# Linear attention and a token MLP mixed by a gate: a new order of the first loads, and of VectorE's first statistics

## The chip, the cores and the metric

One core of one Trainium2 chip runs the kernel. The metric is the device time of one execution in microseconds. All times in the profile count from the start of the profiled span.

## The reference

x is [1, 2048, 512] in bfloat16. Two branches read it and a gate mixes them:

```python
g = sigmoid((x * gate_w).sum(-1))
# A: linear attention, 32 heads of 16, phi(t) = where(t > 0, t + 1, exp(t)) + 1e-6
q, k, v = split(x @ wqkv)
o = (phi(q) @ (phi(k)^T v)) / (phi(q) . sum(phi(k)) + 1e-6)
a = o @ wo
# B: MLP over the tokens, after a layernorm over the 512 features
h = (x - mean(x)) / sqrt(var(x) + 1e-5)
u = gelu(einsum("bsd,sf->bdf", h, w1) + b1)      # w1 [2048, 1792]
b = (einsum("bdf,fs->bds", u, w2) + b2)^T        # w2 [1792, 2048]
return g * a + (1 - g) * b
```

The first matmul of B sums over tokens: each tile of 128 tokens of the normalised x meets the 128 rows of w1 that belong to the same tokens.

## The kernel before

Tokens are cut into NT = 16 tiles of 128 (one token for each of 128 partitions). `xr[:, t, :]` holds tile t of x, `xh[:, t, :]` the normalised tile, `w1A[:, t, :]` the first 1024 columns of w1's tile t.

The kernel is written in the order in which each engine is to run (`pin` and `mm` keep program order on every engine, DMA queues included). It begins with stage one of B: for tiles 0 to 11 in turn, eight matmuls (one for each block of 128 columns of `w1A`, `mlp1` through `mm`, line 74) add to eight accumulators `accA`; the last four tiles are then done block by block, each followed by a gelu on ScalarE. After it come k, the sums for the attention, the other six blocks of stage one mixed with q, and last the second matmul of B and the output, tile by tile. TensorE runs 18 warm-up matmuls on a constant before any data is there.

What feeds the first stage:

- **Loads** (`load`, line 124). They go out on SP's queue unless another engine is named; three go out on ScalarE's own queue (ACT) at the start. On ACT: the rows of b1 into `b_rows`, then the first 128 columns of w1's tile 0, then those of tile 1, then a dummy Sqrt (line 137) that brings in the activation table. On SP: x tiles 0 and 1, the other 896 columns of w1's tile 0, then x tile 2, the other 896 columns of w1's tile 1, x tile 3, w1's tile 2, and so on in turns of x and w1. Behind w1's tile 4 come the rows of b2. VectorE clears `b_rows` (line 114) before either bias load.
- **Statistics on VectorE** (lines 194 to 235). For a tile: `ln_bn` (line 197, statistics of 512 columns at once, or of two halves of 256 for tiles 1 to 3), `ln_aggr` (line 200, aggregation; then a Sqrt on ScalarE, line 202, gives `sd`), `ln_apply` (line 208, reciprocal, and line 210, `xh`). The order is interleaved so that VectorE has work while ScalarE makes `sd`: for tiles 1 to 3 the first half's statistics of tile t, then `ln_apply(t - 1)`, the second half's statistics, `ln_aggr(t)`; from tile 4 on the full statistics of t, `ln_apply(t - 1)`, `ln_aggr(t)`. After tile 8 the bias rows are turned into columns on VectorE (line 232).

Of the kernel before, what the change touches and what calls it, by code (L numbers as in the profile page):

```python
# [15 lines left out]
def kernel(  # L16
# [13 lines left out]
    nc = tc.nc  # L30
    P = nc.NUM_PARTITIONS
# [7 lines left out]
    S, D = X.shape  # L39
    F = B_w1.shape[1]  # L40
    NT = S // P
    ND = D // P
    NF = F // P
# [4 lines left out]
    FA = NFA * P  # L48
    TAIL = 4

    x_view = X.rearrange("(t p) d -> p t d", p=P)
    o_view = O.rearrange("(t p) d -> p t d", p=P)
    wqkv_view = A_wqkv.rearrange("(k p) n -> p k n", p=P)
    w1_view = B_w1.rearrange("(t p) f -> p t f", p=P)
    w2_view = B_w2.rearrange("(f p) s -> p f s", p=P)
    b1_view = B_b1.rearrange("(f p) -> f p", p=P)
# [9 lines left out]
    def ptile(shape, dt, name):  # L66
        return persist.tile(shape, dt, name=name, tag=name)
# [9 lines left out]
    xr = ptile([P, NT, D], BF16, "xr")  # L77
# [17 lines left out]
    b_rows = ptile([32, P], BF16, "b_rows")  # L95
# [22 lines left out]
    w1A = wpool.tile([P, NT, FA], BF16, name="w1A", tag="w1st")  # L118
# [4 lines left out]
    def load(o, i, eng=None, **kw):  # L123
        pin((eng or nc.sync).dma_start(out=o, in_=i, **kw))  # L124

    def load_x(t0, t1):
        load(xr[:, t0:t1, :], x_view[:, t0:t1, :])

    def load_w1a(t):
        load(w1A[:, t, :], w1_view[:, t, 0:FA])  # L130


    tbl = work.tile([P, 1], FP32, name="tbl", tag="tbl", bufs=2)
    load(b_rows[0:NF, :], b1_view, nc.scalar)
    load(w1A[:, 0, 0:P], w1_view[:, 0, 0:P], nc.scalar)
    load(w1A[:, 1, 0:P], w1_view[:, 1, 0:P], nc.scalar)
    pin(nc.scalar.activation(out=tbl[:], in_=eps_t[:], func=ACT.Sqrt))

    load_x(0, 1)
    load_x(1, 2)  # L140
    load(w1A[:, 0, P:FA], w1_view[:, 0, P:FA])
    for t in range(1, NT):
        if t + 1 < NT:
            load_x(t + 1, t + 2)
        if t == 1:
            load(w1A[:, 1, P:FA], w1_view[:, 1, P:FA])
        else:
            load_w1a(t)
        if t == 4:
            load(b_rows[NF : NF + NT, :], b2_view)  # L150
    load(gw_b[:], gw_row_view.to_broadcast([P, D]))
    load(wk_sb[:], wqkv_view[:, :, D : 2 * D])
# [41 lines left out]
    def ln_bn(t, d0, d1, h, parts):  # L194
        if h == 0:
            stats[t] = work.tile([P, parts, BS], FP32, name="stats", tag=f"stats{parts}", bufs=4)
        pin(nc.vector.bn_stats(out=stats[t][:, h, :], in_=xr[:, t, d0:d1]))  # L197

    def ln_aggr(t):
        pin(nc.vector.bn_aggr(out=mv[:, t, :], in_=stats[t][:]))  # L200
        pin(
            nc.scalar.activation(
                out=sd[:, t : t + 1], in_=mv[:, t, 1:2], func=ACT.Sqrt, bias=eps_t[:], scale=1.0
            )
        )

    def ln_apply(t):
        pin(nc.vector.reciprocal(out=rstd[:, t : t + 1], in_=sd[:, t : t + 1]))
        pin(
            nc.vector.tensor_scalar(  # L210
                out=xh[:, t, :], in0=xr[:, t, :],
                scalar1=mv[:, t, 0:1], scalar2=rstd[:, t : t + 1],
                op0=ALU.subtract, op1=ALU.mult,
            )
        )

    HALVES = 4
    ln_bn(0, 0, D, 0, 1)
    ln_aggr(0)
    for t in range(1, NT):  # L220
        if t < HALVES:
            ln_bn(t, 0, D // 2, 0, 2)
            ln_apply(t - 1)
            ln_bn(t, D // 2, D, 1, 2)
        else:
            ln_bn(t, 0, D, 0, 1)
            ln_apply(t - 1)
        ln_aggr(t)
        if t == NT // 2:

            for p in range(0, P, 32):
                pin(nc.vector.transpose(out=b_cols[p : p + 32, :], in_=b_rows[:, p : p + 32]))
            pin(nc.vector.tensor_copy(out=b1_sb[:], in_=b_cols[:, 0:NF]))
            pin(nc.vector.tensor_copy(out=b2_sb[:], in_=b_cols[:, NF : NF + NT]))
# [322 lines left out]
    t = NT - 1  # L557
# [35 lines left out]
```

## Time and profile before

| | |
|---|---|
| time, median of 3 runs | 162.82 us (162.81 to 162.83) |
| the profiled execution: span from its first to its last instruction | 161.6 us |
| TensorE matmul busy | 157.1 us, 97% of the span |
| VectorE busy | 118.7 us, 73% |
| ScalarE busy | 53.0 us, 33% |
| mean TensorE clock granted | 0.998 |

The profile gives the span as the profiled execution's own time; the median of the runs is 1.2 us above it. Engines in the profile: PE is TensorE's matmuls, PEld its weight loads, DVE VectorE, ACT ScalarE, SPq and ACTq the queues on which SP and ScalarE issue DMAs. A duration of an issue (0.43 us for most) is that of the instruction that issues; the data lands later, and the page gives the time from the start of the issue to the landing. The chain of waits is followed back from the last instruction, at each step to what released it.

### The profile page before, as it was taken

The page shows a single profiled execution, that of the slowest core. Times are in us where ns is not written, and L with a number is a line of the kernel's source. Part 1 is how long each engine was busy: PE and PEld are TensorE (multiplying, and loading weights), DVE is VectorE, ACT ScalarE, POOL GpSimd, SP SyncE. Part 2 cuts the span into 40 slices and gives each one's busy share as a digit, 9 for nine tenths or more (in the row PEclk, how much of TensorE's full clock was granted, in tenths as well). Part 3 has the DMA queues.
Part 4 walks back from the last instruction along what each step waited for, and adds up shares of the span by engine and source line. Part 5 has one row for each costly group of instructions (what it writes and reads, how often), then busy time and mean ns, then how long its engine had stood idle before and what let it go on. Part 6 is the DMA issues. An engine that isn't in the chain of part 4 may idle for free.

```text
span 161.6 us, 2275 instructions
## 1 busy us (share of the span) xinstructions
PE 157.1 (97%) x820; PEld 72.9 (45%) x820; DVE 118.7 (73%) x279; ACT 53.0 (33%) x89; POOL 1.2 (1%) x8
## 2 busy tenths in 40 slices
PE   7899999999999999999999999999999999999993
PEld 5344444444444444444444444444444444444452
DVE  2799998959998998799895999999999980000002
ACT  3122226895243221435225970000008300550050
POOL 2000000000000000000000000000000000000000
PEclk9999999999999999999999999999999999999999
DMA  4999998444699540229953007826535925824421
GB/s 140 271 320 353 364 300 144 101 103 106 159 394 390 149 129 0 87 50 310 402 200 67 0 32 230 322 65 143 186 89 136 353 70 143 265 63 105 143 97 32
DMA packets 36966, 28.33 MB, mean 175 GB/s; under 512 B 20572, under 2 KB 31452, under 8 KB 36956
## 3 DMA queue, kind: packets, MB, share of 16 engines
q1 hardware_dynamic: 36368, 27.87, 57.0%
q10 hardware_dynamic: 588, 0.33, 0.7%
q8 instruction: 6, 0.10, 0.3%
q14 instruction: 4, 0.03, 0.1%
HBM read 19.28 MB, written 4.46 MB: 147 GB/s over the span
## 4 chain that ended last, share of the span: by engine, by line
PE 94%; DMA 3%; SPq 1%; DVE 0%; issue 0%; DVEq 0%
PE yps L74 39%; PE accA L74 16%; PE accB L74 13%; PE qacc L74 9%; PE Gps L74 9%; PE kacc L74 9%; DMA w1A<-in_B_w_dram 3%; SPq L124 1%; PE kvps L74 0%; DVE ot L537 0%; PE w2ps L74 0%; DVEq L537 0%
## 5 line engine op out<-in xcount | busy, mean ns | idle before, releaser
L74 PE MATMUL yps<-uT,w2h 128*128 128x512 bf16 (+2 forms) x238 | 49.2, 366 | 0.0
L74 PEld LDWEIGHTS <-w2h 128*128 128x128 bf16 x238 | 22.8, 98 | 25.9
L74 PE MATMUL accA<-xh,w1A 128*128 128x512 bf16 x128 | 28.0, 379 | 0.8 <-DVE xh L210 0.5
L530 ACT ACTIVATE ot<-yps,c,c 128x512 bf16<-128x512 f32 x15 | 11.6, 777 | 46.9 <-PE yps L74 35.5
L74 PE MATMUL accB<-xh,w1B 128*128 128x512 bf16 x96 | 21.5, 379 | 0.0
L537 DVE TENSOR_SCALAR ot<-yps,c,c 128x384 bf16<-128x384 f32 (+1 forms) x2 | 1.1, 545 | 25.5 <-PE yps L74 25.5
L74 PEld LDWEIGHTS <-w1A 128*128 128x128 bf16 x128 | 12.5, 98 | 16.1 <-DMA w1A<-in_B_w_dram 1.4
L74 PEld LDWEIGHTS <-xT 128*128 128x128 bf16 x128 | 12.4, 98 | 14.9 <-issue 0.2
L74 PE MATMUL kacc<-wk_sb,xT 128*128 128x512 bf16 x64 | 15.8, 379 | 0.0
L74 PE MATMUL Gps<-pk,xr 128*128 128x512 bf16 x64 | 15.8, 379 | 0.0
L74 PE MATMUL yps<-W2sb,pqT 128*128 128x512 bf16 (+2 forms) x68 | 14.6, 366 | 0.0
L74 PEld LDWEIGHTS <-w1B 128*128 128x128 bf16 x96 | 9.4, 98 | 11.3
L74 PE MATMUL qacc<-wq_sb,xT 128*128 128x512 bf16 x64 | 14.5, 379 | 0.0
L286 ACT ACTIVATE e<-qacc 128x512 bf16<-128x512 f32 x16 | 9.6, 597 | 12.2 <-DVE kvbdT L434 4.6
L286 ACT ACTIVATE e<-kacc 128x512 bf16<-128x512 f32 x16 | 9.2, 598 | 12.7 <-DVE pk L293 6.8
L197 DVE BATCH_NORM_STATS2 stats<-xr 128x6 f32<-128x512 bf16 (+1 forms) x19 | 11.1, 586 | 2.7 <-DMA xr<-in_A_x_dram 2.7
L288 DVE TENSOR_SCALAR e<-e 128x512 bf16<-128x512 bf16 x32 | 9.2, 288 | 4.6 <-ACT e L286 4.3
L406 DVE SCALAR_TENSOR_TENSOR pq<-pq,odds,rd 128x512 bf16<-128x512 bf16 x16 | 12.0, 752 | 0.6
L402 DVE TENSOR_REDUCE den<-prod 128x32 f32<-128x544 f32 x16 | 11.5, 720 | 0.6
L293 DVE SCALAR_TENSOR_TENSOR pk<-kacc,e 128x512 bf16<-128x512 f32 x16 | 11.1, 692 | 1.0
L293 DVE SCALAR_TENSOR_TENSOR pq<-qacc,e 128x512 bf16<-128x512 f32 x16 | 11.1, 692 | 0.6
L245 DVE CUSTOM_DVE_ANT_0 junk<-xr,gw_b 128x512 bf16<-128x512 bf16 x16 | 11.0, 689 | 0.4
(52 smaller groups left out, 95.0 us busy)
## 6 DMA issues: line engine op xcount, KB each, us to landing
w2h<-in_B_w_dram SPq DMA_DIRECT2D x3, 1792.0 KB, 7.5
w1A<-in_B_w_dram SPq DMA_DIRECT2D x14, 256.0 KB, 4.7
w1B<-in_B_w_dram SPq DMA_DIRECT2D x4, 768.0 KB, 6.2
xr<-in_A_x_dram SPq DMA_DIRECT2D x16, 128.0 KB, 4.1
q_dram<-pq SPq DMA_DIRECT2D x16, 128.0 KB, 3.7
out_dram<-ot SPq DMA_DIRECT2D x15, 128.0 KB, 1.8
w2h<-in_B_w_dram SPq DMA_DIRECT2D x1, 1280.0 KB, 6.5
wk_sb<-in_A_wqkv_dram SPq DMA_DIRECT2D x1, 512.0 KB, 6.5
```

The lines of the kernel that those rows point to most:

```text
L74: nc.tensor.matmul(o, lhsT=lhsT, rhs=rhs, start=start, stop=stop, **kw)
L124: pin((eng or nc.sync).dma_start(out=o, in_=i, **kw))
L197: pin(nc.vector.bn_stats(out=stats[t][:, h, :], in_=xr[:, t, d0:d1]))
L245: nc.vector.tensor_tensor_reduce(out=junk[:], in0=xr[:, t, :], in1=gw_b[:], scale=1.0, scalar=0.0, op0=ALU.mult, op1=ALU.add, accum_out=gp ...
L286: pin(nc.scalar.activation(out=e[:], in_=acc[:], func=ACT.Exp))
L288: nc.vector.tensor_scalar(out=e[:], in0=e[:], scalar1=1.0, scalar2=PHI_EPS, op0=ALU.min, op1=ALU.add)
L293: nc.vector.scalar_tensor_tensor(out=o, in0=acc[:], scalar=0.0, in1=e[:], op0=ALU.max, op1=ALU.add)
L402: pin(nc.vector.tensor_reduce(out=den[:], in_=prod[:], op=ALU.add, axis=AX.X))
L406: nc.vector.scalar_tensor_tensor(out=heads, in0=heads, scalar=odds[:, t : t + 1], in1=rd[:].unsqueeze(2).to_broadcast([P, NH, HEAD]), op0= ...
L530: nc.scalar.activation(out=ot[:, d0:d1], in_=yps[:, d0:d1], func=ACT.Identity, scale=c1[:, t : t + 1], bias=c2[:, t : t + 1],)
L537: nc.vector.tensor_scalar(out=ot[:, d0:d1], in0=yps[:, d0:d1], scalar1=c1[:, t : t + 1], scalar2=c2[:, t : t + 1], op0=ALU.mult, op1=ALU.add,)
```

## The change

Four edits, all in the first loads and in the order of the first statistics:

- x tile 0 comes as two halves: tokens 64 to 127 on ACT's queue, first there, in the place of the b1 rows; tokens 0 to 63 first on SP's queue.
- On SP the 896 columns of w1's tile 1 are issued ahead of x tile 2; the order behind is as it was (x tile 3, w1 tile 2, x tile 4, ...).
- The b1 rows are issued on SP, behind w1's tile 4 and ahead of the b2 rows.
- On VectorE, tile 1 is finished (`ln_apply(1)`) ahead of tile 2's statistics, and these are taken over all 512 columns at once. The first half of tile 3's statistics is still ahead of `ln_apply(2)`.

The instructions of TensorE, ScalarE (but for the first DMA) and GpSimd are as before and in the same order; VectorE has one instruction less.

```diff
-    load(b_rows[0:NF, :], b1_view, nc.scalar)
+    HP = P // 2
+    load(xr[HP:P, 0, :], x_view[HP:P, 0, :], nc.scalar)
     load(w1A[:, 0, 0:P], w1_view[:, 0, 0:P], nc.scalar)
     load(w1A[:, 1, 0:P], w1_view[:, 1, 0:P], nc.scalar)
     pin(nc.scalar.activation(out=tbl[:], in_=eps_t[:], func=ACT.Sqrt))
 
-    load_x(0, 1)
+    load(xr[0:HP, 0, :], x_view[0:HP, 0, :])
     load_x(1, 2)
     load(w1A[:, 0, P:FA], w1_view[:, 0, P:FA])
-    for t in range(1, NT):
+    load(w1A[:, 1, P:FA], w1_view[:, 1, P:FA])
+    load_x(2, 3)
+    for t in range(2, NT):
         if t + 1 < NT:
             load_x(t + 1, t + 2)
-        if t == 1:
-            load(w1A[:, 1, P:FA], w1_view[:, 1, P:FA])
-        else:
-            load_w1a(t)
+        load_w1a(t)
         if t == 4:
+            load(b_rows[0:NF, :], b1_view)
             load(b_rows[NF : NF + NT, :], b2_view)
@@
     ln_bn(0, 0, D, 0, 1)
     ln_aggr(0)
     for t in range(1, NT):
-        if t < HALVES:
+        if t == 2:
+            ln_apply(t - 1)
+            ln_bn(t, 0, D, 0, 1)
+        elif t < HALVES:
             ln_bn(t, 0, D // 2, 0, 2)
             ln_apply(t - 1)
             ln_bn(t, D // 2, D, 1, 2)
```

## The prediction

> **What bounds the kernel now.** I read the chain of waits first, then the list of waits of the first 20 us, then the timeline and the DMA issues of that stretch. Columns of the chain: start, duration, what.
>
> ```profile
> 2.67 4.65 DMA w1A<-in_B_w_dram
> 7.32 0.04 issue
> 7.37 25.86 PE accA L74 x119
> 33.23 4.32 PE kacc L74 x20
> ```
>
> From 7.37 us the chain holds nothing but TensorE until the last tile is finished. So the end is 7.37 plus work that the change leaves alone, and a shift of the first stage shifts the end one for one. Ahead of 7.37 stands one transfer: the last 896 columns of w1's tile 1 (call it w1/1), issued at 2.67, landed at 7.32. What TensorE can win is seen in its waits (total, times, longest):
>
> ```profile
> DVE stats L197 <- DMA xr<-in_A_x_dram: 2.7, 2, 1.9
> ...
> PEld L74 <- DMA w1A<-in_B_w_dram: 1.4, 2, 0.8
> ...
> PE accA L74 <- DVE xh L210: 0.5, 1, 0.5
> ...
> PE accA L74 <- DMA w1A<-in_B_w_dram: 0.3, 1, 0.3
> ```
>
> Two holes: 0.50 before the first matmul (normalised tile 0) and 0.31 at tile 1 (w1/1), 0.81 together; no version of this stage can win more. The timeline shows how close the next tiles are:
>
> ```profile
> 4.95 2.10 PE L74 MATMUL accA<-xh,w1A 128*128 128x512 bf16 x9 [0.50 <-DVE xh L210]
> ...
> 5.27 0.21 DVE L200 BATCH_NORM_AGGREGATE mv<-stats 128x2 f32<-128x12 f32 x1
> 5.44 0.43 DVE L197 BATCH_NORM_STATS2 stats<-xr 128x6 f32<-128x256 bf16 x1
> 5.51 0.30 ACT L202 ACTIVATE sd<-mv,eps_t 128x1 f32<-128x1 f32 x1 [1.26 <-DVE mv L200]
> 5.84 0.16 DVE L208 RECIPROCAL rstd<-sd 128x1 f32<-128x1 f32 x1
> 6.04 0.41 DVE L210 TENSOR_SCALAR xh<-xr,mv,rstd 128x512 bf16<-128x512 bf16 x1
> ...
> 7.75 0.43 DVE L197 BATCH_NORM_STATS2 stats<-xr 128x6 f32<-128x256 bf16 x1 [0.72 <-DMA xr<-in_A_x_dram]
> 8.10 0.15 DVE L208 RECIPROCAL rstd<-sd 128x1 f32<-128x1 f32 x1
> 8.28 0.41 DVE L210 TENSOR_SCALAR xh<-xr,mv,rstd 128x512 bf16<-128x512 bf16 x1
> ```
>
> A matmul takes 25.86/119 = 0.217, eight of them one tile. Tile 2 begins seven matmuls after 7.37, at 8.89, and its xh is ready at 8.28 + 0.41 = 8.69: 0.20 of room. The row at 7.75 says why so late: VectorE stood 0.72 for x tile 3, with tile 2's normalisation behind it in order. The statistics of tile 2 had started at 5.44, because x tile 2 (issued 2.20, 3.2 to landing) was in at 5.40. So the arrival of w1/1 sets the end, with tile 2's xh 0.20 behind it. The DMA rate shows why w1/1 took 4.65 us (window; busy of PE, PEld, DVE, ACT, POOL; PE clock, DMA share, GB/s):
>
> ```profile
> 4.50:5.00 0.50, 0.05 (x1) 0.10 (x1) 0.50 (x2) 0.00 (x0) 0.00 (x0) 1.00 0.96 114
> 5.00:5.50 0.50, 0.50 (x3) 0.29 (x3) 0.47 (x3) 0.00 (x0) 0.00 (x0) 1.00 0.41 144
> ```
>
> The rate falls from 298 GB/s (4.0 to 4.5) to 114 and 144, then climbs to 348 by 7.0 to 7.5. The packet records name the transfer: on most of the 16 engines one packet of w1/1 took 0.3 to 1.2 us instead of 0.07. Its completions on the 16 engines run from 5.22 to 6.73 for fifteen of them, and to 7.32 for the last, which was some 0.6 late in the transfers before it too.
>
> **The change part by part.** All sums are on the profiled execution's span of 161.6; the median of the runs is 162.82, 1.2 more for what lies outside the span, which the change leaves alone.
>
> *x tile 0 in halves.* The ACT half issues near 0.80, as SP's first transfer does: ACT's first issue stood at 1.02 only because the bias load waited for the memset of b_rows (0.87 to 0.98). ACT's three issues then cost 3 x 0.43 + gaps, ending near 2.2 instead of 2.54, and the Sqrt table load with its dummy (2.58 to 4.07) ends near 3.7, so it no longer holds the first sd (3.98, when its mean and variance were there at 3.83). Tile 0 landed at 2.90. Two halves on the same engines land no later than that if ACT's queue is as quick as SP's (2.1 us from issue), and at best 0.3 sooner, half its packets' 0.6; I take 2.75. From landing to first matmul: 0.02 + statistics to aggregation 0.73 (2.92 to 3.65) + aggregation to reciprocal 0.57 (5.27 to 5.84) + 0.20 + normalise 0.41 + 0.05 = 1.98. First matmul 4.73 instead of 4.95 (4.58 to 4.88). Its weight block, issued 0.4 sooner on ACT, comes near 4.4 (was 4.8). But the second block needs the rest of w1's tile 0, landed at 1.72 + 3.3 = 5.02 and unmoved: second matmul near 5.06, was 5.17. Worth 0.11, and with 4.88 still 0.11. The Trainium skill (DMA: Bandwidth & Descriptors, Rules for kernel authors) says that halves of the partitions in two transfers share the same engines and serialise, so are not worth it; by that the first matmul stands at 4.88 and the second stays at 5.06; no row of before has such halves.
>
> *w1/1 ahead of x tile 2.* w1/1 issues at 2.20 and has 128 KB less before it. On the engines that finish last, x tile 2 came 0.4 after the transfer ahead of it (5.02 to 5.40); w1/1 lands that much sooner, 7.32 - 0.40 = 6.92. The second matmul at 5.06 plus eight is 6.80, so TensorE waits 0.15 and goes on at 6.97: 0.40 gained on 7.37. Tile 1's xh, now without a statistics instruction between, is ready near 6.2 and needed at 6.58.
>
> Now x tile 2. It takes the place where w1/1 was: the same bytes are in front of it and itself together. So it lands where w1/1 landed, 7.32, and x tile 3 stays at 7.75. Bounds: 6.73 (the fifteen engines of w1/1) and 7.75; I take 7.30, where the slowest engine put that many bytes before.
>
> *VectorE.* Tile 1 is finished first, then full statistics of tile 2, aggregation, the first half of tile 3, and only then tile 2's normalisation. Everything in that queue now stands behind x tile 2. From its landing to TensorE it is the same 1.98 (half statistics of tile 3, 0.10 + 0.42, fit into the 0.57 while ACT makes sd): 7.30 + 1.98 = 9.28. By x tile 3 it would be 7.75 + 0.99 (7.75 to 8.69 plus 0.05) = 8.74, no bound. TensorE would be ready for tile 2 at 6.97 + 7 x 0.217 = 8.49, so it waits 0.79 there: tile 2 at 9.28 against 8.89, **0.39 later**. Tile 3 would be wanted at 11.02; its aggregation comes 0.78 after tile 2's normalisation starts (8.28 to 9.06), so 9.60, and the normalised tile 1.28 on (9.06 to 10.34), 10.88: no second wait. Tile 4 has 0.8 more room.
>
> *Bias rows.* One issue of 0.36 moves to SP behind w1 tile 4 and pushes the later issues by some 0.4. They are read at 15.06; the neighbour b2 row, issued at 6.18, took 4.3. The next x tile (7.34 + 3.4 = 10.74) is read at 11.53 and TensorE wants tile 6 at 15.84 while xh is there at 13.87. Nothing; if the cover were gone, 0.4.
>
> Sum: -0.40 (w1/1 sooner) + 0.79 (new wait at tile 2) = +0.39; 162.82 + 0.39 = 163.21, given as 163.2.
>
> **The rivals.** *The burst of slow packets does not come back.* It lies in w1/1's packets, which now meet other neighbours; fewer came with w1's tile 0 and hardly any with tile 2. Without it w1/1 takes on the slow engine 0.40 x 224/128 = 0.70 after 5.02, so 5.72, x tile 2 6.12, tile 2 ready at 8.10. Then only the weights of tile 0 bind: tile 1's second matmul at 6.80, tile 2 at 8.32, 0.57 sooner: 162.25. It decides from x tile 2's landing: even at 8.89 - 1.98 = 6.91, faster by 0.33 below 6.58 (x tile 3 then must be in by 7.57). Against it: three runs within 0.02 us, so the burst is no chance event in this order of loads. The Trainium skill (DMA: Bandwidth & Descriptors, Specifications) gives an HBM limit of about 358 GB/s per core; at that rate the 896 KB through x tile 2 take an estimated 2.6 us, and it is in before 5, which is this case. The trace speaks against a steady rate here: 114 and 144 GB/s at 4.5 to 5.5.
>
> *The burst stays, the one late engine is on time.* Then x tile 2 lands at about 6.73 and tile 2 starts at 8.71: 0.18 sooner, 162.64; between 6.58 and 7.24 the change is not to be told from none.
>
> *The ACT half is late.* ACT's weight blocks took 3.1 us; at 0.80 + 3.1 = 3.90 the first matmul is at 5.88, sixteen on tile 2 begins at 9.35: +0.46, 163.28. It decides where it lands after some 3.8.
>
> **How the numbers follow.** 0.2% is 0.33 us, about what can be told from no change. Forecast (x tile 2 later than 7.24): 0.45. ACT half late: 0.04. Burst gone: 0.30. Between: 0.21. Slower 0.49, same 0.21, faster 0.30. The forecast's own range is 163.15 (at 7.24) to 163.65 (x tile 2 at 7.75). The whole: below to 162.2, which takes in the case without the burst, above to 163.5, which leaves out the last of the forecast's own.
>
> **What would show it.** Right: TensorE's second hole shrinks and a new one of 0.8 stands at tile 2, released by xh; VectorE waits for x tile 2 until 7.3, and the chain of waits begins with a transfer of x instead of w1. Wrong: x tile 2 in before 6.9, no dip of the DMA rate at 4 to 5.5, or a hole at tile 0 of over 0.5.

## The result and the profile after

The changed kernel takes 163.43 us (median of 22 runs, 163.16 to 165.58); the kernel before, on the same chips, 162.87 (22 runs, 162.78 to 163.56). The ratio is 1.0029, 95% interval 1.0016 to 1.0042: slower by 0.3%, 0.5 us. The forecast was 163.2 and slower. Direction and size came out; the place did not, as the profile shows at once. A run more than 1.5% above the fastest of its kernel counts as slow and is left out of a ratio; below, that is one run in each of two experiments (165.74 and 166.6).

One correction comes first. The results list span and time of each execution, and they differ by 1.7 to 1.8 us (161.1 beside 162.83 for the kernel before, 163.8 beside 165.58 after), not by 1.2. So the profiled execution of before, span 161.6, was itself some 0.5 us longer than the three runs at 162.8. And the profiled execution of after is the longest of its 22 runs, by 1.6 us. Its waits of the first 20 us (total, times, longest):

```profile
PEld L74 <- issue: 3.5, 11, 0.8
DVE stats L198 <- DMA xr<-in_A_x_dram: 2.7, 2, 2.3
...
PE accA L74 <- DVE xh L211: 0.8, 1, 0.8
```

The hole at tile 1 behind w1's tile 1 is gone, as forecast; no hole at tile 2 has taken its place; the hole ahead of the first matmul has grown from 0.5 to 0.8. New are ten of the eleven waits of the weight loads for nothing that the profile names; the profile of before has only the first, ahead of the warm-up. The timeline of the same execution (rows of SP's and ACT's issues, of VectorE and of TensorE, in order of time):

```profile
0.80 1.45 SPq L124 DMA_DIRECT2D xr<-in_A_x_dram  x2
0.80 0.55 ACTq L124 DMA_DIRECT2D xr<-in_A_x_dram  x1
...
2.31 0.89 SPq L124 DMA_DIRECT2D w1A<-in_B_w_dram  x2
...
3.32 0.69 DVE L198 BATCH_NORM_STATS2 stats<-xr 128x6 f32<-128x512 bf16 x1 [2.33 <-DMA xr<-in_A_x_dram]
...
4.63 0.43 DVE L198 BATCH_NORM_STATS2 stats<-xr 128x6 f32<-128x256 bf16 x1 [0.39 <-DMA xr<-in_A_x_dram]
...
5.62 9.67 PE L74 MATMUL accA<-xh,w1A 128*128 128x512 bf16 x34 [0.78 <-DVE xh L211]
...
6.00 0.15 PEld L74 LDWEIGHTS <-w1A 128*128 128x128 bf16 x1 [0.28 <-issue]
...
6.43 0.15 PEld L74 LDWEIGHTS <-w1A 128*128 128x128 bf16 x1 [0.28 <-issue]
...
7.04 0.69 DVE L198 BATCH_NORM_STATS2 stats<-xr 128x6 f32<-128x512 bf16 x1
```

Three things are to be read here.

- **Issues.** SP's first two took 0.87 together before; now they take 1.45 (0.57 and 0.82 with a gap), and the rest of w1's tile 0 is issued at 2.31 instead of 1.72. x tile 0 is in at 3.2 (its statistics start at 3.32), not 2.9. x tile 1 is in at 4.6, not 3.3, and holds VectorE until 4.63, with tile 0's normalisation behind it in the queue. The first matmul starts at 5.62, 0.67 later than before.
- **x tile 2** (issued 3.24, 3.5 us to landing) is in by 6.76, and its statistics start at 7.04 right behind tile 1's normalisation, without a wait. Its xh is ready at 8.91 (8.50 + 0.41); at full pace TensorE would have come to tile 2 at 5.62 + 16 x 0.216 = 9.08.
- **Half pace.** From 6.00 on one weight load follows the other every 0.427 us, where the kernel before has 0.216, and each takes 0.15 instead of 0.10. Nine data matmuls (those of stage one, as against the warm-up) go at this pace, about 1.9 us; with the 0.2 from the late start (9.08 against 8.89 at tile 2) this makes the 2.2 us between the two spans. The page's clock column reads 1.00 there all the same; only the spacing shows it. Warm-up matmuls, with 256 columns, stand 0.213 apart at first in all profiles: half pace too, since the last ones of before stand 0.11 apart. TensorE starts slow and changes once. The change came at 3.9 in the profile of before, still among the warm-up matmuls, and at 9.6 here. None of the other 21 runs can have had all of these 1.9 us: the longest of them is 163.97, and 1.9 less would be under every run of either kernel.

The Trainium skill (TensorE: Matmul & The Clock Gate, section on the HAM clock gate) has this as a clock gate that starts at half rate and opens after a busy window of some 3.4 us that runs freely, so that the switch falls elsewhere in each execution; the two times above and those of the runs below agree. It names idle gaps of over 3.4 us as the danger, but for an engine that already runs at full rate; what a shorter hole does before that, the runs below show.

### The profile page after: what moved, and what is told of

Same layout as the page of the kernel before. It is cut to its first block, busy times and chain, and to the rows that moved or that the text cites. A ratio compares the mean times of both kernels' runs of the same rounds, so it can differ in the third digit from the quotient of the medians.

```text
span 163.8 us, 2263 instructions
## 1 busy us (share of the span) xinstructions
PE 158.5 (97%) x806; PEld 73.5 (45%) x820; DVE 118.8 (73%) x278; ACT 53.1 (32%) x89; POOL 1.2 (1%) x8
## 4 chain that ended last, share of the span: by engine, by line
PE 89%; DVE 3%; DMA 3%; SPq 2%; issue 1%; DVEq 0%
PE yps L74 38%; PE accA L74 13%; PE accB L74 13%; PE kacc L74 8%; PE qacc L74 8%; PE Gps L74 8%; DMA xr<-in_A_x_dram 3%; SPq L124 2%; DVE stats L198 1%; DVE xh L211 1%; PE kvps L74 0%; DVE ot L541 0%; DVE mv L201 0%; PE w2ps L74 0%; DVE rstd L209 0%
## 5 line engine op out<-in xcount | busy, mean ns | idle before, releaser
L74 PE MATMUL accA<-xh,w1A 128*128 128x512 bf16 x126 | 29.6, 397 | 0.9 <-DVE xh L211 0.8
L74 PEld LDWEIGHTS <-w1A 128*128 128x128 bf16 x128 | 13.0, 102 | 17.5 <-issue 2.7
```

Source lines behind the costliest of these rows:

```text
L74: nc.tensor.matmul(o, lhsT=lhsT, rhs=rhs, start=start, stop=stop, **kw)
```

## The experiments

Theory I: the halves make SP's issues slow, and x tile 0 late. Theory II is the prediction's: x tile 2, behind w1's tile 1, makes a hole at tile 2. Theory III: a hole ahead of the first data matmul keeps TensorE at half pace.

**The changed kernel again** (no edit).

> The changed kernel again, for a second profile. Theory I (issue): SP and ACT issuing at the same time slow each other, so SP's first two issues take 0.57 and 0.82 us instead of 0.40 and 0.41, x tile 0 lands near 3.3 instead of 2.9, the first matmul is at 5.6, and TensorE then runs on without a hole at tile 2; about 163.2 to 163.8. Theory II (the prediction): first matmul at 4.6 to 5.1 and a hole of 0.8 at tile 2 behind x tile 2; 163.2.

163.80 (163.15 to 165.74, 11 runs); ratio 1.0051 (1.0026 to 1.0075). The issues take 0.57 and 0.82 again, the first matmul starts at 5.65 after a hole of 0.8, and eight of the first nine data matmuls stand 0.427 apart; this profiled execution took 165.52. x tile 2 was in at 7.2 this time, and TensorE, slow, did not wait. Theory II fails in both profiles.

**x tile 0 whole, the rest as changed.**

```diff
-    load(xr[HP:P, 0, :], x_view[HP:P, 0, :], nc.scalar)
-    load(xr[0:HP, 0, :], x_view[0:HP, 0, :])
+    load_x(0, 1)
```

> The change without the halves: x tile 0 whole on SP, ACT's first issue is w1's first block at once; the rest as changed. Theory I: the two queues still issue side by side, SP's second issue still takes about 0.8, x tile 0 lands at 3.1 or later, and the time stays at 163.2 to 163.6. If it is the halves themselves that cost: issues back at 0.41, x tile 0 at 2.9, 162.3 to 162.8. Theory II: the halves are worth nothing, the hole at tile 2 stays, 163.2.

163.13 (162.85 to 163.69, 12 runs), ratio 1.0002 (0.9988 to 1.0016): the loss is gone, but the 162.3 to 162.8 expected in this case is not reached.

```profile
0.79 0.90 ACTq L124 DMA_DIRECT2D w1A<-in_B_w_dram  x2
0.79 0.87 SPq L124 DMA_DIRECT2D xr<-in_A_x_dram  x2
...
4.97 5.89 PE L74 MATMUL accA<-xh,w1A 128*128 128x512 bf16 x23
```

Both queues issue side by side from 0.79 on, and neither is slow. So theory I in its first form, two queues at once, is wrong; the halves themselves cost.

**The halves alone.** The kernel before, with the diff's two half loads in place of the whole one and the b1 rows behind w1 tile 4.

> The kernel before with the halves alone (the b1 rows go behind w1 tile 4, since their place on ACT is taken); w1's tile 1 and VectorE in the old order. Theory I: the whole SP stream comes 0.58 later, first matmul at 5.6, w1's tile 1 at 7.9 instead of 7.32, +0.5 to +0.6, 163.4. Theory II: the halves end behind w1's tile 0 and tile 1 as before; no difference, 162.8.

163.52 (163.24 to 164.09, 12 runs), ratio 1.0021 (1.0007 to 1.0036).

```profile
5.27 5.50 PE L74 MATMUL accA<-xh,w1A 128*128 128x512 bf16 x24 [0.43 <-DVE xh L212]
...
7.35 3.14 PEld L74 LDWEIGHTS <-w1A 128*128 128x128 bf16 x16 [0.47 <-DMA w1A<-in_B_w_dram]
```

First matmul at 5.27, not 5.6: SP's second issue took 0.57 here and not 0.82, x tile 1 was in at 3.9, and VectorE did not wait for it. w1's tile 1 came at 7.3 and not at the 7.9 expected: its place in the old order was not moved by the late issues, only the start was.

**Both halves on SP.** Is it the two queues, or the 64 partitions?

```diff
-    load(xr[HP:P, 0, :], x_view[HP:P, 0, :], nc.scalar)
     load(xr[0:HP, 0, :], x_view[0:HP, 0, :])
+    load(xr[HP:P, 0, :], x_view[HP:P, 0, :])
```

> The changed kernel with both halves of x tile 0 on SP, one behind the other; ACT begins with w1's first block. Theory I (two queues that issue halves at the same time slow each other): each half issues in 0.41 or less, x tile 1 in 0.41. Theory Ia (a transfer of 64 partitions is slow to issue, wherever): 0.55 to 0.6 for each half and over 0.5 for what follows. In both x tile 1 and all behind it are one issue later than with x tile 0 whole, first matmul at 5.2 to 5.6, 163.1 to 163.6.

SP alone, two halves and x tile 1:

```profile
0.80 1.84 SPq L124 DMA_DIRECT2D xr<-in_A_x_dram  x3
2.69 0.43 SPq L124 DMA_DIRECT2D w1A<-in_B_w_dram  x1
```

0.58, 0.57 and 0.58, while ACT's two issues of 128 partitions in the same stretch took 0.39 and 0.45. So here an issue of 64 partitions takes 0.57 where one of 128 takes 0.39 to 0.45, and on SP the issue behind the halves, x tile 1 whole, is slow as well. The second half was in at 4.15 only; the first matmul came at 6.20, not at the 5.2 to 5.6 expected, after a hole of 1.36, and theory III is seen again: eight data matmuls at half pace, 165.84 for this execution. Four runs gave 163.88 to 166.6, over the 163.1 to 163.6 expected; ratio 1.0113 (1.0043 to 1.0183, without the longest).

**Halves by columns.** 128 partitions and 256 columns on each queue.

```diff
-    load(xr[HP:P, 0, :], x_view[HP:P, 0, :], nc.scalar)
-    load(xr[0:HP, 0, :], x_view[0:HP, 0, :])
+    load(xr[:, 0, HD:D], x_view[:, 0, HD:D], nc.scalar)
+    load(xr[:, 0, 0:HD], x_view[:, 0, 0:HD])
```

> The changed kernel with x tile 0 cut by columns instead of tokens: all 128 partitions, 256 columns on each queue. Theory I: side by side issue again takes 0.55 and 0.8, first matmul at 5.6, 163.4 to 163.8. Theory Ia: with 128 partitions each issue takes 0.41 to 0.46, SP's third issue starts at 1.7, x tile 0 is in by 2.9 to 3.1, first matmul near 5.0, 162.8 to 163.2.

163.44 (163.01 to 163.87, 12 runs), ratio 1.0018 (1.0002 to 1.0034). Issues of 0.39 and 0.41 again, so among these first loads the slow issue goes with the number of partitions; x tile 0 in at 3.0 and the first matmul at 4.98, as expected. It is no rule for later loads: the bias rows, 14 and 16 partitions, took 0.32 to 0.39 wherever they stood on SP behind w1's tile 4, while b1's 14 took 0.63 first on ACT. Why is open. The time is over the range given. In its profile the pace changed at 6.8 only, after four slow data matmuls, and x tile 2 held VectorE for 0.41; how much of the loss the other runs owe to either, I can't tell. Splitting x tile 0 in this way brings it no sooner than 2.9 either.

**The new order alone.** The kernel before with w1's tile 1 ahead of x tile 2 and VectorE's new order; x tile 0 whole, the b1 rows first on ACT.

> The kernel before with the new order alone: w1's tile 1 ahead of x tile 2 and VectorE's tile 1 first; x tile 0 whole, b1 rows first on ACT as before. Theory I: SP's issues at 0.41 again, first matmul at 4.95, w1's tile 1 near 6.9, and the time is better than before by up to 0.4, 162.4 to 162.7, if x tile 2 is in by 6.6. Theory II: hole at tile 2, x tile 2 lands at 7.3, +0.4, 163.2.

162.94 (162.78 to 163.56, 12 runs), ratio 0.9991 (0.9976 to 1.0007), not the 162.4 to 162.7 expected. The timeline:

```profile
4.96 5.92 PE L74 MATMUL accA<-xh,w1A 128*128 128x512 bf16 x26
...
6.62 0.69 DVE L196 BATCH_NORM_STATS2 stats<-xr 128x6 f32<-128x512 bf16 x1 [0.16 <-DMA xr<-in_A_x_dram]
...
8.09 0.41 DVE L209 TENSOR_SCALAR xh<-xr,mv,rstd 128x512 bf16<-128x512 bf16 x1
```

One unbroken row of matmuls from 4.96; w1's tile 1 was in at 5.4 (forecast 6.9), x tile 2 at 6.6 (forecast 7.3). From 6.62 it is 1.94 to tile 2's first matmul at 8.56, as the 1.98 of the prediction had it, against 8.89 before. Run again:

> The new order alone again (w1's tile 1 ahead of x tile 2, VectorE's tile 1 first; x tile 0 whole, b1 rows first on ACT). If the order helps whenever w1's tile 1 is late in the old one: mean 0.1 to 0.3 below the kernel before, the fastest executions equal at 162.8. If not: the same mean.

162.98 (162.81 to 163.67, 12 runs), ratio 0.9992 (0.9976 to 1.0008). Twice the means lie 0.14 to 0.15 below the kernel before (163.04 against 163.19, 163.07 against 163.21), twice the interval holds 1, and the shortest executions are the same (162.78 and 162.81 against 162.83 and 162.79). It is the best version tried, by less than can be told. The second profile has a hole, too:

```profile
4.95 5.23 PE L74 MATMUL accA<-xh,w1A 128*128 128x512 bf16 x23 [0.62 <-DVE xh L209]
```

Yet not one data matmul behind these 0.62 us is slow, 23 in 5.23. The pace had changed at 3.7, among the warm-up matmuls and ahead of the hole. So theory III can only be meant of a hole that comes while TensorE is still slow.

**The loads without VectorE's edit.** The kernel of the new order, with VectorE's order of before.

> The kernel before with w1's tile 1 ahead of x tile 2 alone; VectorE's order as before, x tile 0 whole, b1 rows first on ACT. The first half of tile 2's statistics now stands ahead of tile 1's normalisation and waits for x tile 2. If that lands at 6.6 as in the run with both edits: tile 1's xh at 7.6, tile 1 starts 0.9 later than TensorE could, tile 2 at 9.3, +0.4, 163.2 to 163.4. If VectorE's edit does nothing: as that run, 162.8 to 163.0.

163.24 (162.88 to 163.89, 10 runs), ratio 1.0006 (0.9989 to 1.0023).

```profile
6.05 0.43 DVE L196 BATCH_NORM_STATS2 stats<-xr 128x6 f32<-128x256 bf16 x1 [0.57 <-DMA xr<-in_A_x_dram]
```

VectorE now waits for x tile 2 with tile 1's normalisation behind it: the mechanism expected, but x tile 2 was in at 6.0 and not 6.6, the wait 0.57, and TensorE lost little (tile 1 at 7.04, where 6.75 + 0.22 = 6.97 was possible). VectorE's edit is worth at most what an interval of this width hides.

**The hole closed.** The changed kernel with 21 warm-up matmuls.

```diff
-    for _ in range(18):
+    for _ in range(21):
```

> The changed kernel with 21 warm-up matmuls instead of 18, so that TensorE is busy until about 5.5 where its warm-up runs at half rate (213 ns each). Theory III (clock): in the profiles of the changed kernel the idle 0.8 us ahead of the first data matmul lets TensorE run its first nine data matmuls at 427 ns instead of 216 (1.9 us); with the hole closed they run at 216 from 7 us at the latest, the executions at 165.5 are gone, and the median comes down to 163.0 to 163.4. Without theory III: as the changed kernel, 163.4 to 163.8, some at 165.5.

In the profile one slow data matmul instead of nine, and no run of 12 over 164.52. But the median is 163.91 (163.53 to 164.52), ratio 1.0044 (1.0026 to 1.0061), not the 163.0 to 163.4 expected. In this execution TensorE also waited once near 129 for w2, which only one other profile has (the next one):

```profile
129.60 2.49 PEld L74 LDWEIGHTS <-w2h 128*128 128x128 bf16 x13 [0.57 <-DMA w2h<-in_B_w_dram]
```

It costs 0.24. With the first matmul at 5.28 instead of 4.95, and 0.12 at the end that comes with the split load (see below), this is 0.69 of the 0.76 by which the median lies over the kernel before; whether every run has the wait for w2, no trace shows. The run fits a slow pace that goes with the hole; it does not show that closing it this way pays.

**A hole made.** The kernel before with 14 warm-up matmuls, all loads as they were.

```diff
-    for _ in range(18):
+    for _ in range(14):
```

> The kernel before with 14 warm-up matmuls instead of 18, and nothing else changed: a hole of 0.9 us or more ahead of the first data matmul, x tile 0 as before at 2.9. Theory III (clock): the idle stretch lets TensorE's first data matmuls run at 427 ns in some executions, nine or more of them, as in the changed kernel; some executions at 164.5 or more, where the kernel before has none over 164.0. If the idle stretch does not matter: as the kernel before, 162.8 to 163.9, since data matmuls start at 4.95 in both.

165.06 (163.68 to 165.52, 6 runs), ratio 1.0098 (1.0061 to 1.0136): 1.6 us for four warm-up matmuls left out.

```profile
2.71 1.27 PE L74 MATMUL warm_ps<-const-bfloat16-1.0 128*128 128x256 bf16 x5
4.95 5.02 PE L74 MATMUL accA<-xh,w1A 128*128 128x512 bf16 x13 [0.97 <-DVE xh L210]
```

The first data matmul is at 4.95 as before, and thirteen then take 5.02, which is 0.39 each. The weight loads stand 0.427 apart from 5.33 to 9.17. This is theory III with nothing else changed in the kernel: a hole of 0.97 us, far under 3.4, while TensorE is still slow, is enough to keep it slow for some 4 us more. Not all of it is the pace: of the 2.1 us between this span and that of before, some 0.5 come near 131.5, where TensorE waits 0.34 for w2. The least that one of the six runs lost is 0.6 (163.68 against 163.1).

## Why the prediction was right or wrong

- **x tile 0's landing, "I take 2.75" (bounds 2.6 to 2.9), first matmul 4.73: wrong, and here the loss begins.** It was 3.2, and 5.62. The condition it rested on, that ACT's queue is as quick as SP's, held (0.55 and 0.57); that a half issues as quickly as a whole did not. The trace of before had a hint that I read as something else: ACT's b1 row load, 14 partitions, took 0.63 to issue. The halves alone cost 0.21%, the change without them 0.02%.
- **x tile 1 is missing from that sum.** Of the 0.67 by which the first matmul is late, x tile 0 makes 0.30 (tile 0's `sd` is there at 4.56 instead of 4.26). The other 0.37 is x tile 1, issued behind a half in 0.82 and landed at 4.60 instead of 3.34, with tile 0's normalisation behind its statistics. With x tile 1 in time (the halves alone, and the run with 21 warm-up matmuls) the first matmul stood at 5.27 and 5.28.
- **0.12 at the end is missing, too.** From the end of the last weight load to the end of the span it is 3.10 to 3.12 in the six profiles with x tile 0 in two pieces, 2.99 to 3.00 in the six with it whole. What the six have and the others have not is one DMA more (129 issues instead of 128); how this comes to bear on the end is open. With it the shortest executions add up: the halves alone have 163.24 against 162.83, that is 0.41, and 0.32 for the late start plus 0.12 is 0.44; the columns have 163.01, that is 0.18, and 0.03 plus 0.12 is 0.15. The changed kernel's shortest is 0.38 over that of before. This is argued, since none of these shortest executions was profiled.
- **The rival "the ACT half is late"** named the right place and a price of 0.46, with 4 chances in 100; its cause was wrong, since ACT's half was in at 2.9 to 3.0 in both profiles of the changed kernel and SP's at 3.2 to 3.3.
- **The Trainium skill's rule** (DMA: Bandwidth & Descriptors, Rules for kernel authors) that halves of the partitions are not worth it holds, but x tile 0 came 0.3 to 0.4 later, not at the same time. The issue costs 0.17 more each; the rest of the delay is not explained.
- **w1's tile 1, "7.32 - 0.40 = 6.92": too late.** 6.2 and 6.0 in the two profiles of the changed kernel, 5.3 to 5.7 in the three profiles of the new order with x tile 0 whole and the b1 rows on ACT. **x tile 2 "where w1/1 landed", 7.30: too late, if within the bounds.** 6.8 and 7.2 in the same two, where it was issued 0.57 later than the sum had it, 6.6 with the order alone. Slow packets stand in each profile, but at other places, on x tile 2 itself in the order alone (its packets took 0.5 to 1.0 us near 5.2). The dip of the rate did not come back in the changed kernel: 379, 291 and 234 GB/s from 4.0 to 5.5 in steps of 0.5, where the profile of before had 298, 114 and 144. So the rule that the same bytes ahead take the same time failed, since the slow packets belong to no fixed transfer. This was the rival "between" in the landing, with its 0.2 of gain.
- **The new wait of 0.79 at tile 2: absent** in the changed kernel, since TensorE came later and the data sooner. The 1.98 from landing to matmul was right to 0.04. Of the three signs of being wrong, the hole at tile 0 (0.8) and the missing dip came in both profiles, x tile 2 before 6.9 in one.
- **The gain of 0.40 at w1's tile 1: seen in profiles, not found in the times.** With the order alone tile 2 began at 8.56 and 8.51, against 8.89 before. But the order alone gives 0.15 at the mean, within its interval. The shortest executions of both orders agree, 162.8, beside a span of 161.1; that is 0.5 less than the profile of before, about the hole at tile 1 (its second matmul came at 7.37, where 6.68 + 0.22 = 6.90 was possible). So I read the hole as one of some executions and not of all; this is argued, since none of the shortest executions of the old order was profiled. It is no chance of one profile, either: w1's tile 1 came at 7.3 again in the halves alone, and at 6.9 with 14 warm-up matmuls, both in the old order.
- **"The end shifts one for one": right** but for the pace, the 0.12 and a wait for w2 in two profiles. The term that was missing altogether is the half pace, which hardly showed in the one profile of before (3.9, within the warm-up). It makes the spread of 162.8 to 163.7 plausible for the kernel before, too: in five profiles of other kernels with the first data matmul at 4.95 to 4.98 the pace changed at 3.7, 5.3, 5.6, 6.6 and 6.8, and the times of these executions are 162.92, 162.96, 163.17, 163.62 and 163.83.
- **The bias rows: nothing, right.** They had landed well before their use, and moved no wait in the changed kernel; the change without the halves, with its bias rows moved, is at 1.0002.

So the number was near by luck: a loss of 0.79 that did not come less a gain of 0.40 that the times do not show, in place of, by the shortest executions, a first tile that is late by 0.3 and an end that is late by 0.1. The slow TensorE behind the late tile is what makes the profiled executions so long; how often the others have a part of it is not known.

## What to carry to other kernels

Count a split load by its issues before its bytes: two halves that issue slower than the whole bring the tile later, and what stands behind them on the queue with it. A fill at the start of a kernel that ends too early can cost more than it looks (1.6 us where four matmuls were left out), though a longer one did not pay here; measure the pace of the first data matmuls by their spacing, not by a column of clocks. And take one profile of a stage that ends on a transfer as one draw: its hole may not be in the other executions.

## What the runs showed of the hardware that was not expected

- Among the first loads an issue of 64 partitions of 1 KB took 0.55 to 0.58 us on SP and on ACT, one of 128 partitions with none of these ahead of it on its queue 0.38 to 0.46, of 256 columns or 512; the issue behind a half on the same queue took 0.57 to 0.85.
- A hole of 0.8 to 1.4 us ahead of the first data matmul, with TensorE still slow, was followed by eight to ten matmuls at half pace in four profiles (5.62, 5.65, 6.20 and 4.95 their starts). In the other eight, with holes of up to 0.62, there were none to four; in the two of these with over 0.43 the pace had changed before the hole.
- The time at which the pace changed ran from 3.7 to 9.6 us over the profiles, with the same 0.84 for the first warm-up matmul: 3.7 to 6.8 in those eight, 9.2 to 9.6 in those four.
- A kernel with one load more ended 0.12 us later behind its last weight load, in six profiles against six.
